# Scaled queries and a negated maximum for four blocks, and a new order of all engines, in windowed attention with a feed-forward network

## The chip, the cores and the metric

The kernel runs on one core of a Trainium2 chip, in one launch. The metric is the device time of one execution in microseconds (us), lower being better. The engines of a core work side by side, each through its own list of instructions in order: PE (TensorE: matmuls), DVE (VectorE), ACT (ScalarE), POOL (GpSimd) and SP (SyncE, which here only issues transfers). They wait for each other by semaphores.

## The reference

Attention with a sliding window of 128 keys and four sink keys, over 4 batches, 8 heads, 768 positions and 64 elements a head; its output, 3072 tokens of 512 elements, goes through a network of two layers.

```python
scores = scale * np.matmul(q, k.transpose(0, 1, 3, 2))     # scale = 1/sqrt(64)
keep = is_sink | in_window          # pos < 4, or 0 <= query - key < 128
scores = np.where(keep, scores, -1000000000.0)
scores = scores - np.max(scores, axis=-1, keepdims=True)
a = np.exp(scores)
a = a / (np.sum(a, axis=-1, keepdims=True) + 1e-09)
x = np.matmul(a, v)                 # then (4*768) x 512, heads side by side
h = x @ w_in                        # 512 x 2048
g = h * (1.0 / (1.0 + np.exp(-1.702 * h)))
out = g @ w_out                     # 2048 x 512
```

## The kernel before

The queries are cut into 24 blocks of 128, six to a batch; block b is the (b mod 6)-th of its batch. Blocks 0, 6, 12 and 18 are the first of their batches: they see one block of keys, their own, which contains the sinks. Every other block sees its own keys, those of the block before, and the four sinks. The blocks are worked on in the order 0, 6, 12, 18 and then the rest.

**Loads.** POOL issues the loads of q, k, v and of the two weight matrices (four slices each, `wi0` to `wi3` and `wo0` to `wo3`), which also cast float32 to float16. SP and ACT issue the loads of small constants: the identities `ident` and `identb`, the mask `bias0`, the mask `later`, and rows of v for the sinks (`vsa`). From `vsa`, `vsb` is made, one product for each batch (L344).

**A first block, step by step.** TensorE transposes q and k (`tq`, `tk`, L383), and DVE or ACT cast the results from PSUM into `qkT` (`cq`, `ck`). Four matmuls of `identb` with `bias0` write the mask into the PSUM buffer of the scores (`msk`, L464), and eight add the scores (`sc`, L478). DVE takes the maximum of each row (`mx`, L545), multiplies it by -scale (`nb`, L557), and ACT computes the exponential straight from PSUM with that bias, four instructions for each half of the heads (`bx`, L568). TensorE transposes the probabilities (`ta`, L650), they are copied (`ca`), multiplied with v, which has a column of ones (`av`, L710), normalised by DVE (`nm`, a reciprocal and a product, L722 and L723), transposed (`tx`, L740) and copied into `xT` (`cx`). The sinks' keys of a batch are copied out of `qkT` by DVE (`ks`, L446).

**The other blocks.** The mask is a predicated copy by DVE (`pk`, L535); the maximum is subtracted by DVE (`sb`, L582), and ACT takes one exponential for all heads out of SBUF (`ex`, L606). The sinks' scores come from matmuls of their own (`snk`, L507). From the fifth block on, q and k, the probabilities (`at<-a`, L681) and the attention output (`xT<-xn`, L753, called `txd`) are mostly transposed by DMA, issued by SP, and POOL separates the probabilities of the two key blocks (L637).

**The network.** Blocks form the groups [0], [6], [12, 18], and then pairs. For each group the first layer is computed in tiles (`h`, L786) and passed through the activation: for the first three groups by a tanh on ACT and a product on DVE (L800, L807), for the rest by one table function on ACT (`g`, L816). Where ACT goes from exponentials to this function or back, it loads a table (ACT_TABLE_LOAD). The second layer (`o`, L836) is copied from PSUM (`osb<-o`, by ACT or DVE) and stored by SP (L856). The last block is put out in two parts, of 320 and 192 columns.

**Buffers and order.** In PSUM three buffers (`mm`) serve all transposes, `hT` and `o`, two the scores and one `av`. Every step is an entry of a plan, and a list of numbers, ORDER, holds the sequence in which the steps are given to the engines; a letter behind a number chooses the engine where a step may run on several (d, a, p, s for DVE, ACT, POOL, SP). Each engine, and each engine's DMA queue, follows this sequence; nothing is decided while the program runs.

```python
    def emit(self, order):
        letter = {"d": DVE, "a": ACT, "p": POOL, "s": SP}
        ...
            op.emit(choice) if len(op.eng) > 1 else op.emit()
```

Of the kernel before, what the change touches and what calls it, by code (L numbers as in the profile page):

```python
# [40 lines left out]
LH = 1.0  # L41
HW = set()
LD4 = 0.65
LD, LW, QKX, ATX, XTX, STX, SPX2 = 0.97, 2.55, 1.55, 1.56, 0.77, 0.85, 1.9
AHEAD = 4
TQ = set(BLOCKS[:8])
# [5 lines left out]
RING = dict(RING,qkn=7)  # L52


ORDER = """
1a 9 6 8d 100 15 4a 5a 11 14 7 96 0a 23 94 21 3s 98 17 2s 29 18 104 107 105a 101p 102 103d 16 108 171 20 109 150 19
172a 10 95d 125 110 24 112 225 111 99d 26 151a 113 126d 27 114 115 97d 88 127 106 128a 130 92 226d 116a 117 12 90 129
148 118a 119 13 131 149a 22 120 194 132 121 86 196 195a 135 173 197a 87 133 122 134 89 123 199 124a 200 138 30 136 613
139d 137 25 152 142 174a 140 143 153 614 141d 615 154 91 144 155 619 156 145 157 158 146 616 93 620 147d 159 160 621
637 32 617 634 638 618 176 639 635 631 36 175 636 177 632 610 178 633 161 611 181 35 628 162a 179 612 180 163 182 165  # L60
622 164d 166 629 184 183 33 167 623 185d 168 39 198 630 169 31 204 640 170a 205 188 227 189 641 228a 201 28 230 186
206 642 231 209 202 624 187a 203 215 190 38 643 208 191 207 229 216d 210 644a 192 217 235 211 43 193a 625 232 212a 236
41 280 282 626a 256 281d 258 213 283a 627 233 652 259a 214 237 257a 649 653 218 238 234 261 661 241 40 650 262 654 239
285 37 260 651 662 242 286 304 44 655 266 243a 263 34 219 656 646 663 42 657 658 647 244 220 664 648 659 245 267 670
45 665 660 240 221 671 264 268 246 672 247a 269 265 248 667 222 270 249 666 250 284 668 271 251 48 676 669 46 290 252
323 673 47 253 287 677 291 254 306 272 678 288 255a 674a 223 292 679 273 224a 293 289 682 680d 294 51 307 305 683 50
688 295 308 311 49 686 309 675 52 684 687 312 689 692 310 685 313 276 693 690 314 277 296 315 704 297 344 324 345 705
327 691 316 53 330 325 694 326 361 331 274 695 696 275 328 698 697 681 332 278 317 699 279a 333 329 298 334 318 343
299 700 346 54 347 300 706 55 349 335 701 57 301 350 302 645 319 303a 707 348 702a 352 351 716 708a 320 353 362 336
321 717 354 720 322 337 365 724 709 59 721 363 399 714 364 368 60 712 715 703 369 725 722 366 713 340 355 723 710 341  # L70
367 718 711 356 371 370 338 719 732 64 339 372 726 342 56 733 62 382 381 373 61 383 727 387 384 359 734 360 385 728
388 401 735 390 386 729 374 419 389 750 402 391 375 730d 400 736d 751 748 392 67 406 403 742 66 404 752 65 743 407 749
740 63 753 378 738 379 408 376 739 744 377 393 409 357 405 745 746 358 741 394 420 380 747 439 58 410 754 440 423 421
760 422 426 397 755 427 411 398 761 424 457 756 425 762 428 757 429 430 412 766 758d 438 759 413 767 763 431 444 69
441 770 737 442 71 768 771 445 72 764a 772 769 446 68 416 443 773 780 432 447 417 788 781 433 448 414 774 415 73 458
459 789 775 460 449 464 395 778 396 461 776 418 779 465 782 777 462 436 495 450 783 463 466 790 75 765 437 731 784 467
74 468 434 451 785 435 476 791 482 786d 800 792a 479 454 793 801 798 469 455 794 514 452 795 802 453 808 803 456 477
804 809 478 470 799 483 796 480 471 806 797 485 805 484 816 76 481 810 77 486 474 80 496 475 817 70 502 807 499 487
497 82 811 498 78 500 818 503 81 516 822 504 819 823 505 517 501 812 820a 506 515 821 824 488 518 813 489 825 507 828
814d 83 472 826 552 473 79 519 832 827 521 829 535 836 833 536 522 492 837 834 508 523 830 524 493 509 520 844 831 84  # L80
835 490 534 525 491 845 540 494 541 838 537 846 526 542 839 538 512 787 847 513 543 840 539 544 553 852 848a 545 527
573 864 853 574 590 528 510 841 511 865 559 860 842d 529 546 861 556 862 530 850 547 554 854 851 555 85 560 531 855
856 532 557 858 533 857 561 866 859 558 550 815 562 591 563 551 872 597 867 863 592 564 873 593 598 868 843 594 548
849 880 595 869 596 881 600 565 888 599 549 874 889 870d 566 601 886 875 884 876a 602 567 885 572 568 878 877 575 569
879 892 570 578 882 571 893 603 576 887 890 579 604 894 891 577 883 900 580 581 895 582 901 607 912 608 583 896 913
605 871 897 606 902 898a 910 584 916 911 585 914 917 918 915 908 919 906 909 586 907 903 587 922 588 920 589 923 609
921 904a 928 924 929 925 930 926d 946 931 947 934 942 935 932a 948 943 933 940 905 927 936 941 899 938 937 949 944 939
956 945 950 957 951 958 952 962 953 963 954a 959 964 955 960d 965 961 966d 967
# [67 lines left out]
def kernel(  # L156
# [72 lines left out]
    z_s = plan.add("zs", DVE, 0.25, lambda: nc.vector.memset(vsa, 1.0), key=-897)  # L229
    z_a = [  # L230
# [133 lines left out]
    for pos, b in enumerate(BLOCKS):  # L364
# [5 lines left out]
        qkb = qkT[:, SLOT[b]]  # L370


        buf, n, unit = tunit[b]
        if b in OCT:
            parts = []
            before = used_slot.pop(SLOT[b], [])
            for w in (1, 0):
                tp = ps("mm", (P, 8, 4, 16), FP32, f"t{'qk'[w]}{b}")

                def t_qk(w=w, buf=buf, n=n, tp=tp):  # L380
                    for t in range(8):
                        for l in range(2):
                            nc.tensor.matmul(  # L383
                                tp()[64 * l : 64 * l + 64, t], buf()[:, n, w, t],
                                ident.rearrange("p (j l u) -> p l j u", l=2, u=16)[:, l], start=True, stop=True,
                            )
# [5 lines left out]
                parts.append(  # L392
                    plan.add(
                        f"c{'qk'[w]}{b}", {DVE: 0.6, ACT: 0.5}, 0,
                        lambda e, w=w, tp=tp, qkb=qkb: copy(
                            e, qkb[:, 4 * w : 4 * w + 4].rearrange("p c (u t) -> p c u t", t=8),
                            tp().rearrange("p t c u -> p c u t"),
                        ),
                        deps=[a] + before, give=[tp], key=K0 - 40,
                    )  # L400
                )
            o_qkt[b] = parts
        elif b in TQ:
# [3 lines left out]
            for w in (1, 0):  # L407

                def t_qk(w=w, buf=buf, n=n, tp=tp):
                    src = buf()[:, n, w].rearrange("p h d -> p (h d)")  # L410
                    for c in range(4):
                        nc.tensor.transpose(tp()[:, 4 * w + c], src[:, bass.ts(c, P)], ident)

                a = plan.add(
                    f"t{'qk'[w]}{b}", PE, 0.25 if early else 0.226, t_qk, deps=[ld["qk"[w], b], o_ident],
                    take=[tp], give=[buf], key=K0 - 40,
                )
                parts.append(
                    plan.add(
                        f"c{'qk'[w]}{b}", {DVE: 0.36, ACT: 0.49}, 0,  # L420
                        lambda e, w=w, tp=tp, qkb=qkb: copy(e, qkb[:, 4 * w : 4 * w + 4], tp()[:, 4 * w : 4 * w + 4]),
                        deps=[a] + before, give=[tp], key=K0 - 40,
                    )
                )
# [16 lines left out]
        if r == 0:  # L441

            def sink_keys(bb=bb, qkb=qkb):
                for hl in range(2):
                    rows = slice(64 * hl, 64 * hl + 64)
                    nc.vector.tensor_copy(  # L446
# [3 lines left out]
            o_ks[bb] = plan.add(f"ks{b}", DVE, 0.45, sink_keys, deps=o_qkt[b] + [z_k], key=K0 - 10)  # L450
# [79 lines left out]
        for hf in range(2):  # L530
# [12 lines left out]
            def rowmax(hf=hf, t=sc[hf], own=own, small=small, ms=ms):  # L543
                part = small[:, 4 * hf : 4 * hf + 4].rearrange("p (j l) -> p l j", l=2)
                nc.vector.tensor_reduce(out=part, in_=t()[:, :, :, own], axis=AX.X, op=ALU.max)  # L545
# [154 lines left out]
        for hf in range(2):  # L700
# [34 lines left out]
        if b in TX:  # L735
# [163 lines left out]
```

## Time and profile before

| | |
|---|---|
| time, median of 3 runs | 233.0 us (232.78 to 233.21) |
| profiled execution | 232.43 us |
| its span, first to last instruction | 230.7 us |
| TensorE busy | 217.0 us, 94% |
| VectorE busy | 154.5 us, 67% |
| ScalarE busy | 139.8 us, 61% |
| GpSimd busy | 111.2 us, 48% |
| first matmul starts | 5.68 us |

The profiled execution is one run of the program. An engine counts as busy while it executes, not while it waits, issues a transfer or branches. In rows of groups, the name behind an arrow (`<-`) at the end is what ended the engine's idle time; in the timeline the numbers are the start and the duration in us.

### The profile page before, as it was taken

The page shows a single profiled execution, that of the slowest core. Times are in us where ns is not written, and L with a number is a line of the kernel's source. Part 1 is how long each engine was busy: PE and PEld are TensorE (multiplying, and loading weights), DVE is VectorE, ACT ScalarE, POOL GpSimd, SP SyncE. Part 2 cuts the span into 40 slices and gives each one's busy share as a digit, 9 for nine tenths or more (in the row PEclk, how much of TensorE's full clock was granted, in tenths as well). Part 3 has the DMA queues.
Part 4 walks back from the last instruction along what each step waited for, and adds up shares of the span by engine and source line. Part 5 has one row for each costly group of instructions (what it writes and reads, how often), then busy time and mean ns, then how long its engine had stood idle before and what let it go on. Part 6 is the DMA issues. An engine that isn't in the chain of part 4 may idle for free. (4 is left out here: it accounts for less than half of the span.)

```text
span 230.7 us, 5431 instructions
## 1 busy us (share of the span) xinstructions
PE 217.0 (94%) x2202; PEld 151.6 (66%) x2202; DVE 154.5 (67%) x388; ACT 139.8 (61%) x220; POOL 111.2 (48%) x129
## 2 busy tenths in 40 slices
PE   0878899999999999999999999999999999999994
PEld 0666865876586686486577496486686686775863
DVE  2487899999979976987797848668577847121001
ACT  2278774874597687168378386786358486631531
POOL 8983435995393869077392619265350312300000
PEclk9999999999999999999999999999999999999999
DMA  5999999999999899999999989999647542402312
GB/s 76 167 189 200 206 198 180 168 134 91 153 182 168 159 242 131 148 162 135 165 196 136 196 172 131 131 185 110 140 92 114 142 99 45 99 0 45 114 71 91
DMA packets 120904, 32.07 MB, mean 139 GB/s; under 512 B 112016, under 2 KB 117936, under 8 KB 120880
## 3 DMA queue, kind: packets, MB, share of 16 engines
q0 software_dynamic: 69888, 13.64, 72.2%
q1 hardware_dynamic: 50512, 17.96, 38.7%
q8 instruction: 17, 0.28, 0.5%
q10 hardware_dynamic: 480, 0.13, 0.3%
q14 instruction: 7, 0.06, 0.1%
HBM read 27.46 MB, written 6.29 MB: 146 GB/s over the span
## 5 line engine op out<-in xcount | busy, mean ns | idle before, releaser
L786 PE MATMUL hT<-xT,w_in 128*128 128x256 f16 (+1 forms) x832 | 93.2, 264 | 1.5 <-ACT gT L816 0.5
L836 PE MATMUL o<-w_out,gT 128*128 128x512 f16 (+2 forms) x400 | 92.1, 371 | 0.0
L786 PEld LDWEIGHTS <-w_in 128*128 128x128 f16 x832 | 73.9, 98 | 14.1 <-issue 3.7
L816 ACT ACTIVATE gT<-hT 128x512 f16<-128x512 f32 x80 | 45.8, 597 | 33.1 <-PE hT L786 32.9
L836 PEld LDWEIGHTS <-gT 128*128 128x128 f16 x400 | 36.1, 98 | 33.3 <-issue 1.9
L637 POOL TENSOR_SCALAR_AFFINE_SELECT atp<-at 128x1024 f16<-128x1024 f16 (+1 forms) x22 | 22.3, 1015 | 72.9 <-DMA at<-a 69.9
L545 DVE TENSOR_REDUCE mx<-sc 128x4 f32<-128x512 f32 x48 | 32.7, 683 | 0.8 <-PE sc L478 0.5
L606 ACT ACTIVATE a<-e 128x1056 f16<-128x1056 f32 (+2 forms) x24 | 22.5, 938 | 15.4 <-issue 12.5
L535 DVE COPY_PREDICATED sc<-later,sc 128x512 f32<-128x512 uint16 x40 | 26.8, 689 | 3.6 <-PE sc L483 3.3
L582 DVE TENSOR_TENSOR e<-sc,mx 128x512 f32<-128x512 f32 x40 | 26.7, 684 | 0.7
L722 DVE RECIPROCAL rcp<-av 128x4 f32<-128x4 f32 x48 | 8.6, 179 | 24.0 <-PE av L712 22.1
L637 POOL TENSOR_SCALAR_AFFINE_SELECT at<-at 128x1024 f16<-128x1024 f16 (+1 forms) x22 | 22.2, 1009 | 1.4
L271 POOL DMA_DIRECT2D v<-in_v_dram x24 | 21.7, 906 | 2.0 <-DMA w_in<-in_moe_w_in_dram 1.2
L723 DVE TENSOR_TENSOR xn<-av,rcp 128x256 f16<-128x256 f32 x48 | 20.4, 424 | 1.7
L241 DVE COPY osb<-o 128x512 f32<-128x512 f32 (+2 forms) x10 | 6.3, 634 | 21.2 <-PE o L836 21.1
L606 ACT ACT_TABLE_LOAD x12 | 15.4, 1283 | 6.1 <-DVE e L596 4.0
L318 POOL DMA_DIRECT2D qkn<-in_q_dram x18 | 16.1, 897 | 4.5 <-DMA w_out<-in_moe_w_out_dram 1.6
L816 ACT ACT_TABLE_LOAD x13 | 16.7, 1283 | 2.4 <-PE hT L786 1.8
L318 POOL DMA_DIRECT2D qkn<-in_k_dram x18 | 16.0, 890 | 3.6 <-DMA w_out<-in_moe_w_out_dram 3.4
L710 PE MATMUL av<-v,at 128*128 128x65 f16 x192 | 17.5, 195 | 0.1
L710 PEld LDWEIGHTS <-at 128*128 128x128 f16 x192 | 14.4, 98 | 2.7 <-DVE at L241 0.3
L712 PE MATMUL av<-v,atp 128*128 128x65 f16 x160 | 15.1, 194 | 0.0
(58 smaller groups left out, 198.1 us busy)
## 6 DMA issues: line engine op xcount, KB each, us to landing
out_dram<-osb SPq DMA_DIRECT2D x23, 256.0 KB, 3.2
qkn<-in_q_dram POOLq DMA_DIRECT2D x24, 128.0 KB, 5.7
qkn<-in_k_dram POOLq DMA_DIRECT2D x24, 128.0 KB, 5.4
v<-in_v_dram POOLq DMA_DIRECT2D x24, 128.0 KB, 5.5
w_in<-in_moe_w_in_dram POOLq DMA_DIRECT2D x4, 512.0 KB, 10.4
w_out<-in_moe_w_out_dram POOLq DMA_DIRECT2D x4, 512.0 KB, 15.4
at<-a SPq DMA_TRANSPOSE x18, 3.7
qkT<-qkn SPq DMA_TRANSPOSE x10, 4.3
```

The costliest lines, as they stand in the source:

```text
L271: f"v{b}", POOL, 0.88, lambda b=b, view=view: nc.gpsimd.dma_start(v65[:, b, :, 0:D], view),
L318: lambda buf=buf, n=n, w=w, view=view: nc.gpsimd.dma_start(buf()[:, n, "qk".index(w)], view),
L535: nc.vector.copy_predicated(out=t()[:, :, :, own].rearrange("p l j s -> p (l j) s"), mask=later.unsqueeze(1).to_broadcast((P, 4, P)), data ...
L545: nc.vector.tensor_reduce(out=part, in_=t()[:, :, :, own], axis=AX.X, op=ALU.max)
L582: nc.vector.tensor_tensor(out=e32()[:, 512 * hf : 512 * hf + 512].rearrange("p (l j s) -> p l j s", l=2, j=2), in0=t()[:, :, :, own], in1= ...
L606: nc.scalar.activation(out=a16()[:, lo:hi], in_=e32()[:, lo:hi], func=AF.Exp, scale=scale)
L637: nc.gpsimd.affine_select(out=dst, in_=at()[:, lo : lo + num], pattern=[[0, num], [1 if own else -1, P]], compare_op=ALU.is_ge if own else ...
L710: nc.tensor.matmul(av()[:, i], at()[:, c], v65[:, b, h], start=(r == 0), stop=(r == 0))
L723: nc.vector.tensor_tensor(out=xn()[:, xi, 4 * hf : 4 * hf + 4].rearrange("p (j l) d -> p l j d", l=2), in0=av()[:, :, 0:D].rearrange("p (l ...
L786: nc.tensor.matmul(ht()[:, n].rearrange("p (n t) -> p n t", n=NT), w_in16[:, c, bass.ts(f, P)], t0()[:, i0 : i0 + NT, c], start=(c == 0), ...
L816: lambda fs=fs, gt=gt, ht=ht: nc.scalar.activation(out=gt()[:, fs[0] : fs[-1] + 1], in_=ht(), func=AF.Gelu_apprx_sigmoid),
L836: nc.tensor.matmul(po()[:, 0:width], gt()[:, F, bass.ts(t, P)], w_out16[:, F, c0 : c0 + width], start=(F == 0), stop=(F == NF - 1),)
```

## The change

For the four first blocks the cast of q now multiplies by scale, and the row maximum is written negated into the buffer from which the exponential takes its bias. The eight `nb` steps fall away, and the exponential has a scale of 1. `ks` may run on POOL. A constant tile of ones is set (`zo`), which no step of this kernel reads: the branch for it, a value product with the operands exchanged (AVT), is empty, as is OCTDT's other choice.

All of ORDER is new, and with it the choice of engines. TensorE has the same 328 steps in another sequence. SP issues `identb` and `bias0` before anything else (before, ACT issued them as third and fourth); `later` goes to ACT. `vsb` of batches 0 and 2 and one `ks` go from DVE to POOL; casts and evictions change places between DVE and ACT, so that DVE has 275 steps after 276, ACT 163 after 172, with 30 table loads in the program after 26, and POOL 128 after 125. On TensorE the start reads as follows, before and after (the last figure of `ta`, `av` and `h` is the half or the tile):

```
before: tq0 msk0 tk0 sc0 tk18 tq12 tk6 tk2 ta0_0 tq6 msk6 ta0_1 tk12 av0_0 sc6 tk1 av0_1 tq1 tq18 tx0 snk1 ta6_0 h0_1 ...
after:  msk0 tq0 tk0 sc0 tk18 tk1 tq6 tk6 tq18 msk6 ta0_0 sc6 ta0_1 tq12 tk12 av0_0 av0_1 ta6_1 msk12 ta6_0 tx0 sc12 tk2 h0_1 ...
```

The loads of POOL up to the last slice of `w_out`:

```
before: q0 k0 k18 q12 k6 k2 q6 v0 k12 v6 q18 k1 q1 wi1 wi3 wi2 v12 wi0 wo0 wo1 q2 v18 wo2 wo3
after:  q0 k0 k18 k1 q6 k6 k12 q18 q12 k2 v0 wi1 wi0 v6 q1 v12 wi2 q2 wi3 wo0 wo1 v18 wo2 wo3
```

The last four steps of TensorE were the last part of 320 columns and then that of 192; now the part of 320 columns ends the list, and ACT copies it. The diff, without the numbers of ORDER and the unused branch:

```diff
+OCTDT = "FP32"
+AVT = set()
+NEGATE = True
...
+    ones = const.tile([P, D], FP16, name="ones")
+    z_o = plan.add("zo", DVE, 0.12, lambda: nc.vector.memset(ones, 1.0), key=-890)
...
+        prescaled = NEGATE and b in NB
+        qf = [scale if prescaled else 1.0, 1.0]
...
-                        lambda e, w=w, tp=tp, qkb=qkb: copy(
+                        lambda e, w=w, tp=tp, qkb=qkb, qf=qf: copy(
                             e, qkb[:, 4 * w : 4 * w + 4].rearrange("p c (u t) -> p c u t", t=8),
-                            tp().rearrange("p t c u -> p c u t"),
+                            tp().rearrange("p t c u -> p c u t"), qf[w],
                         ),
...
-            def sink_keys(bb=bb, qkb=qkb):
+            def sink_keys(e, bb=bb, qkb=qkb):
...
-                    nc.vector.tensor_copy(
+                    (nc.vector if e == DVE else nc.gpsimd).tensor_copy(
...
+            def rowmax(hf=hf, t=sc[hf], own=own, small=small, ms=ms, neg=prescaled):
                 part = small[:, 4 * hf : 4 * hf + 4].rearrange("p (j l) -> p l j", l=2)
+                if neg:
+                    nc.vector.tensor_reduce(out=part, in_=t()[:, :, :, own], axis=AX.X, op=ALU.max, negate=True)
+                    return
...
-                    nbias = const.tile([P, 8], FP32, name=f"nb{b}")
+                    nbias = small if prescaled else const.tile([P, 8], FP32, name=f"nb{b}")
...
-                o = plan.add(f"nb{b}_{hf}", DVE, 0.09, neg, deps=[o], key=K0 - 29)
-
-                def bexp(hf=hf, t=sc[hf], own=own, a16=a16, nbias=nbias):
+                if not prescaled:
+                    o = plan.add(f"nb{b}_{hf}", DVE, 0.09, neg, deps=[o], key=K0 - 29)
+
+                def bexp(hf=hf, t=sc[hf], own=own, a16=a16, nbias=nbias, scale=1.0 if prescaled else scale):
```

More of the change, by code (lines that the diff above doesn't have):

```diff
@@ L45 @@
 AHEAD = 4
+AVT = set()
+NEGATE = False
 TQ = set(BLOCKS[:8])
@@ L60 @@
[L60 to L64, printed above, removed]
@@ L420 @@
                         f"c{'qk'[w]}{b}", {DVE: 0.36, ACT: 0.49}, 0,
-                        lambda e, w=w, tp=tp, qkb=qkb: copy(e, qkb[:, 4 * w : 4 * w + 4], tp()[:, 4 * w : 4 * w + 4]),
+                        lambda e, w=w, tp=tp, qkb=qkb, qf=qf: copy(
+                            e, qkb[:, 4 * w : 4 * w + 4], tp()[:, 4 * w : 4 * w + 4], qf[w]
+                        ),
                         deps=[a] + before, give=[tp], key=K0 - 40,
@@ L734 @@
         xt, ti = xts[b]
-        if b in TX:
+        if b in AVT:
+            pass
+        elif b in TX:
             tpx = ps("mm", (P, 4, P), FP16, f"tx{b}")
```

98 lines of the change are left out of this document (65 added, 33 removed).

## The prediction

> **What bounds the kernel now.** The page comes first: what each engine does in the span.
>
> ```profile
> span 230.7 us, 5431 instructions
> PE 217.0 (94%) x2202; PEld 151.6 (66%) x2202; DVE 154.5 (67%) x388; ACT 139.8 (61%) x220; POOL 111.2 (48%) x129
> ```
>
> TensorE works 217.0 of 230.7 us, so 13.7 us are all that a reordering can win; its matmuls are the same 2202 after the change. The profiled execution took 232.43 us, 1.7 beyond its span; the median of the runs is 233.0 (232.78 to 233.21), 0.6 above it. I make the sum against the execution and carry the difference over to the median. The table by stages (columns: stretch and length, then PE, PEld, DVE, ACT and POOL busy, clock, DMA share, GB/s) says where the 13.7 us lie.
>
> ```profile
> 5.77:11.50 5.73, 4.62 (x108) 3.72 (x109) 2.79 (x7) 1.64 (x4) 5.73 (x8) 1.00 1.43 167
> 11.50:17.30 5.80, 4.60 (x76) 3.54 (x76) 4.74 (x14) 4.44 (x13) 5.18 (x8) 1.00 1.36 189
> 17.30:23.00 5.70, 4.95 (x99) 3.83 (x98) 4.32 (x16) 4.69 (x13) 2.01 (x3) 1.00 1.37 200
> 23.00:28.80 5.80, 5.14 (x87) 4.66 (x86) 4.65 (x13) 4.29 (x13) 2.50 (x3) 1.00 1.29 205
> 28.80:34.60 5.80, 5.63 (x80) 4.04 (x74) 5.41 (x15) 4.20 (x12) 1.75 (x2) 1.00 1.42 198
> 60.00:220.00 160.00, 159.05 (x1455) 109.75 (x1454) 105.81 (x262) 102.39 (x136) 71.30 (x73) 1.00 1.04 136
> 220.00:230.70 10.70, 7.65 (x55) 4.87 (x52) 0.85 (x2) 1.75 (x4) 0.00 (x0) 1.00 0.16 58
> ```
>
> TensorE loses 1.11, 1.20, 0.75, 0.66 and 0.17 us in the five stretches up to 34.6 (3.9 in all), 0.95 in the long one, and 3.05 behind its last matmul. The rest lies ahead of its first matmul, where it waits for the first load. Everything that the change can win stands in three numbers, then: start 3.9, middle 0.95, tail 3.05. The start moves 167 to 205 GB/s all along: the loads keep it company and may be its true limit.
>
> **The start, step by step.** Rows of the timeline, those between left out (start, us, engine, line, operation; in brackets the idle time before and what ended it), and of four groups (busy us, mean ns | idle time before, and what ended it):
>
> ```profile
> 2.14 0.75 ACTq L217 DMA_DIRECT2D bias<-cbias  x1
> 5.68 0.64 PE L383 MATMUL tq<-ident,qkn 128*64 128x64 f16 x16 [5.68 <-DMA qkn<-in_q_dram]
> 6.60 1.01 PE L464 MATMUL sc<-bias,identb 128*128 128x256 bf16 x4 [0.28 <-DMA bias<-cbias]
> 7.54 0.64 PE L383 MATMUL tk<-ident,qkn 128*64 128x64 f16 x16
> 8.97 0.61 PE L478 MATMUL sc<-qkT 64*128 64x128 f16 x8 [0.79 <-DVE qkT L241]
> 9.40 0.69 DVE L545 TENSOR_REDUCE mx<-sc 128x4 f32<-128x512 f32 x1 [0.49 <-PE sc L478]
> 11.03 1.14 ACT L568 ACTIVATE a<-sc,nb 128x128 f16<-128x128 f32 x4 [0.26 <-DVE nb L557]
> 20.04 1.05 PE L786 MATMUL hT<-xT,w_in 128*128 128x128 f16 x16 [0.24 <-ACT xT L245]
> 41.51 1.03 PE L836 MATMUL o<-w_out,gT 128*128 128x512 f16 x4
> L557 DVE TENSOR_SCALAR nb<-mx 128x4 f32<-128x4 f32 x8 | 1.7, 208 | 0.0
> L568 ACT ACTIVATE a<-sc,nb 128x128 f16<-128x128 f32 x32 | 9.3, 390 | 2.0 <-DVE rcp L722 1.7 <-DVE nb L557 0.3
> L241 DVE CAST qkT<-tk 128x512 f16<-128x512 f32 x3 | 2.1, 685 | 5.0 <-PE tk L383 4.9
> L239 DVE TENSOR_SCALAR osb<-o 128x512 f32<-128x512 f32 x1 | 0.7, 679 | 0.0
> ```
>
> The arithmetic change itself is small. It removes eight `nb` of 208 ns, 1.7 us of VectorE, and puts nothing in their place, if a maximum that is written negated and a cast that also multiplies cost what they did without (the trace of before shows neither; a copy of the same size that scales is there in one output eviction, 679 ns against the plain cast's 685, so I take 0, with +0.1 us an instruction, eight maxima and four casts, 1.2 us of VectorE, as the far end). On the path the eight are worth far less than 1.7: ScalarE waited for `nb` 0.3 us in all. At the first block 0.94 us lie between the end of the maximum (9.40 + 0.69) and the exponential (11.03), and that gap closes by at most that much.
>
> The order does more. `identb` and `bias0` are now issued by SyncE first of all, not as third and fourth of ScalarE's queue (2.14), and the four mask matmuls stand ahead of `tq0` on TensorE. Where the two constants land before the 5.6 us of q, the mask is paid inside the first wait, and `tk0` starts at 6.22 and not 7.54. Where they land late, the mask delays `tq0` instead; the gain is then near 0.4. I take the early case: `sc0` at 7.73, 1.24 earlier. From there each step waits for something that did not move: the transposes of k of block 18 for a free product buffer, at 10.4, whose cast waits for a load; `tq18` for q's load, 11.9; the mask of block 12 for the exponentials of block 6, 17.3; `tx0` for the cast of q of block 12, 18.4. The first matmuls of the network start at 19.4 against 20.04, with one block's mask and scores more behind them. (These starts come from walking the new order by hand with the rows' durations and the loads in their order.) The loads come in the same number ahead of the last slice of `w_out`, and this one bounds the first output blocks:
>
> ```profile
> 24.04 0.74 POOL L331 DMA_DIRECT2D w_out<-in_moe_w_out_dram  x1 [1.79 <-DMA w_in<-in_moe_w_in_dram]
> ...
> DMA to landing us min/median/max: 14.9/15.4/15.9
> L344 POOL TENSOR_TENSOR vsb<-vsa,ownm 32x520 f16<-32x520 f32 x1 | 1.2, 1227 | 0.0
> ```
>
> It lands at 24.04 + 15.4 = 39.4, and the fourth output tile of block 0 cannot start before; by my chain it starts at 39.85. Before it starts at 41.51, but with one more output tile (0.86 us of spacing) and one set of transposes (0.22) behind it, so that at equal work the new order stands at 40.93: **0.6 us gained** of the 3.9. Behind it the transposes of blocks 4 and 3 wait for casts of q and k, 0.2 given back: **start -0.4**. The two `vsb` products that go to GpSimd take 1.2 us each there and delay the loads issued behind them; as the last slice stands 15.4 us in the queue, the queue does not run dry, and I cost that at 0 (2.5 us of late loads, if it did).
>
> **The middle.** The program loads ScalarE's tables 30 times where it was 26, as some pairs of exponentials are now apart.
>
> ```profile
> L816 ACT ACTIVATE gT<-hT 128x512 f16<-128x512 f32 x80 | 45.8, 597 | 33.1 <-PE hT L786 32.9
> L816 ACT ACT_TABLE_LOAD x13 | 16.7, 1283 | 2.4 <-PE hT L786 1.8 <-PE snk L507 0.3
> 142.04 1.28 ACT L606 ACT_TABLE_LOAD   x1 [1.47 <-issue]
> 146.38 1.03 PE L786 MATMUL hT<-xT,w_in 128*128 128x256 f16 x8 [0.55 <-ACT gT L816]
> ```
>
> Four more loads are 5.1 us of ScalarE by the row, and up to 4 x (1.28 + 1.47) = 11 with the idle time ahead of the load shown. ScalarE waits 32.9 us for `hT`, so that much is covered in sum; if the cover fails at one place, TensorE loses what it lost at 146.38, 0.55 us. One stop in 13 switches of this kind before makes 0.2 for four more. (The Trainium skill, "ScalarE: Activation LUTs", section "What ACT_TABLE_LOAD costs", gives 1283 ns and a drain of about 1380 ns for each switch, and so speaks against this change with 10.6 us of ScalarE. The trace agrees with the first part exactly; for the second it has the 1.47 us of idle time, which stand ahead of the load and not behind it.)
>
> The DMA transposes on SyncE's queue (of the attention output, `txd`) have less TensorE work to hide behind. The one ahead of group 5 shows the danger:
>
> ```profile
> 90.24 1.32 SPq L753 DMA_TRANSPOSE xT<-xn  x1
> 97.52 0.70 PE L786 MATMUL hT<-xT,w_in 128*128 128x256 f16 x5 [0.34 <-DMA xT<-xn]
> xT<-xn SPq DMA_TRANSPOSE x8, 3.1
> ```
>
> It took 7.3 us where the median is 3.1, and cost 0.34. Between the last value product of that group and its first network matmul lie 8.4 us of TensorE work before and 6.0 after (counted in the two orders with the trace's spacings); for the groups after it 8.4 against 7.2 and 8.5 against 5.1. At the median's 3.1, with 0.6 of normalising and up to 0.8 of queue ahead, that is 4.5, and all hold, with 0.6 to 2.7 us left. Around this transpose four loads were issued before, one now. So I drop most of the 0.95 us of stops, leave 0.45 for the new ones and the table loads: **middle -0.5**.
>
> **The tail.** The last output tile is now the one of 320 columns, evicted by ScalarE, not that of 192 by VectorE:
>
> ```profile
> 227.08 0.96 DVE L241 COPY osb<-o 128x320 f32<-128x320 f32 x2 [14.31 <-PE o L836]
> 227.69 0.36 DVE osb L241
> out_dram<-osb SPq DMA_DIRECT2D x23, 256.0 KB, 3.2
> out_dram<-osb SPq DMA_DIRECT2D x1, 96.0 KB, 1.7
> ```
>
> The eviction grows by about 0.1 us, and the store from 96 to 160 KB: between the rows (64 of 160 KB more, of 1.5 us) 0.6, though those of 256 KB met other traffic; I take 0.2 for it, 0.1 to 0.7 in all. **Tail +0.3.**
>
> Sum: -0.4 - 0.5 + 0.3 = -0.6; 231.8 on the execution's footing, **232.4 against the median's 233.0**.
>
> **The rivals.**
>
> *A transpose lands late (slower).* Had the first `txd` taken as long as before, with 6.0 in place of 8.4 us beside it, TensorE would stop 0.34 + 2.4 = 2.7 us instead of 0.34. It decides where a landing passes some 4.5 us from issue. For it: the 7.3 us in the row, three places where up to 40% of the cover is gone. Against: the loads that were issued around it have moved away. Time: 232.4 + 2.7 = 235.1; half of it, 233.8.
>
> *TensorE warms up later (slower).* The same four mask matmuls take 1.03 us at 13.78 and 0.60 at 21.28:
>
> ```profile
> 13.78 1.03 PE L464 MATMUL sc<-bias,identb 128*128 128x256 bf16 x4
> ...
> 21.28 0.60 PE L464 MATMUL sc<-bias,identb 128*128 128x256 bf16 x4
> ```
>
> In the new order TensorE has a gap of about 1 us at 16 to 17 (value products of block 0 wait for a normalisation, the mask of block 12 for exponentials). If that moves the fast state behind the first network matmuls, the mask costs 0.43 more and 16 such matmuls 0.86 more: +1.3, of which the waits absorb little; 233.7. (The Trainium skill, "TensorE: Matmul & The Clock Gate", "What's actually happening", has the clock doubled after a busy window of about 3.4 us whose phase runs free. The change of the row agrees, though the granted clock in the table by stages reads 1.00 throughout; no run here shows the window.)
>
> *The loads bound the start.* Had `w_out` always been the limit, or `bias0` landed late, the 0.4 is gone and the casts' 0.2 stays: 233.0.
>
> *All stops go.* Start -1.0 as several waits close at once, middle -0.95, tail +0.1: 231.1.
>
> That the change brings nothing by its arithmetic alone is part of the forecast: 0.3 us is its whole price on the path.
>
> **How the numbers follow.** Forecast 0.40 (231.8 to 232.9), all stops go 0.12, loads 0.13, late transposes 0.24, late warm-up 0.11. About 0.2%, 0.47 us, is what a measurement of this kernel can tell from no change. Faster by that means under 232.53: three quarters of the forecast's case less a little, all of the second, a little of the third: 0.28 + 0.12 + 0.03 = 0.43. Within: 0.10 of the forecast's and 0.07 of the loads' case and 0.01 of the rest: 0.18. Slower: 0.39. The range reaches from 230.7 (start -1.3, middle -0.95, tail 0) to 235.1, the late transpose in full; 1 in 8 is left out.
>
> **What would show it.** Right: `sc0` near 7.7, the first network matmul near 19.4, the fourth `o` tile of block 0 at 39.4 to 40, no `nb` rows; in the long stretches TensorE idle under 0.5 us; the last store about 0.3 us longer behind its matmul. Wrong: the list of TensorE's waits names `xT<-xn` or `atp` with over 1 us (late transposes), the masks of blocks 12 and 18 both at 1.0 us (late warm-up), or casts of q that take 0.1 us more than the 0.6 to 0.7 of before (a scaling that is not free).

## The result and the profile after

The changed kernel takes 235.6 us (median of 6 runs, 234.48 to 236.27) against 233.1 for the kernel before (232.65 to 233.54): a ratio of 1.0105, 95% interval 1.0077 to 1.0132. It is slower by 1%, where 232.4 was forecast and 235.1 was the end of the range. Run again beside later kernels, it took 236.4 (ratio 1.0144, 1.0104 to 1.0185). Every ratio is to the kernel before, run in the same batch, and is formed from the runs within 1.5% of the fastest of their kernel; where a kernel has others (one run in ten with the stores moved, two in ten with the reductions in the new order), the median given is of all runs and up to 0.3 us higher than theirs.

The page of the changed kernel, first lines:

```profile
span 233.6 us, 5436 instructions
## 1 busy us (share of the span) xinstructions
PE 219.2 (94%) x2202; PEld 153.3 (66%) x2202; DVE 157.2 (67%) x387; ACT 139.9 (60%) x214; POOL 113.6 (49%) x133
```

The span grew by 2.9 us. VectorE has eight instructions of `nb` fewer and yet 2.7 us more busy time. What TensorE waited for, without the first loads and the waits of 0.2 us or less (us in total, times, longest):

```profile
PE hT L835 <- DVE osb L247: 1.3, 1, 1.3
PE tq L391 <- DVE qkT L245: 0.9, 1, 0.9
PE sc L488 <- DVE qkT L247: 0.8, 1, 0.8
PE av L757 <- DVE xn L770: 0.7, 1, 0.7
PE tx L789 <- ACT at L251: 0.5, 1, 0.5
PE hT L835 <- ACT osb L251: 0.5, 1, 0.5
PE av L752 <- DVE ss L530: 0.3, 1, 0.3
```

`xT<-xn` is not among them: no transpose by DMA came late. In their place stand evictions (`osb`) and the sink copy `ss`, which the forecast had not on its list; the other four fall in the start, before 26 us. The two late stops in the table by stages:

```profile
160.00:180.00 20.00, 19.39 (x180) 12.44 (x179) 17.02 (x43) 16.46 (x20) 7.39 (x7) 1.00 0.61 87
180.00:200.00 20.00, 20.00 (x182) 13.69 (x180) 7.34 (x21) 8.70 (x12) 4.37 (x4) 1.00 0.35 61
200.00:220.00 20.00, 18.72 (x144) 13.38 (x141) 2.43 (x5) 6.16 (x12) 0.00 (x0) 1.00 0.33 73
```

To compare orders I use one number, TensorE's delay: the start of a step less the undisturbed spacings of all steps ahead of it (for each kind of step, the median spacing in the trace of before). It grows where TensorE waits or runs at its slow clock, and not with work. Each row is one execution, and these differ: the profiled ones took, from the top, 232.4, 235.4, 236.8, 233.7, 233.9, 232.8 and 231.7 us, and that of the changed kernel with reductions is 2 us faster than its median. From the profiles:

| delay of TensorE, us, at | 45 us | 100 us | 160 us | 227 us |
|---|---|---|---|---|
| before | 13.7 | 15.4 | 17.2 | 17.5 |
| changed | 14.6 | 16.4 | 17.4 | 20.2 |
| changed, run again | 14.2 | 17.4 | 18.4 | 21.7 |
| stores moved up | 13.5 | 16.6 | 17.6 | 18.6 |
| stores and two subtractions moved up | 14.2 | 16.1 | 17.7 | 18.8 |
| changed, with reductions | 14.0 | 15.2 | 16.2 | 17.7 |
| before, with reductions | 14.0 | 15.2 | 16.5 | 16.8 |

So in this execution the 2.9 us are 0.9 up to 45 us, 1.8 from there to 227, and 0.2 behind the last matmul (the span ends 3.23 us behind it, 3.05 before). The 1.8 are a gain and a loss: from 100 to 160 us the delay grows by 1.0 where it grew by 1.8 before, as old stops are gone, and from 160 to 227 by 2.8 where it grew by 0.3.

### The profile page after: what moved, and what is told of

Read it like the earlier page. It is cut to its first block, busy times and chain, and to the rows that moved or that the text cites. A ratio compares the mean times of both kernels' runs of the same rounds, so it can differ in the third digit from the quotient of the medians.

```text
span 233.6 us, 5436 instructions
## 1 busy us (share of the span) xinstructions
PE 219.2 (94%) x2202; PEld 153.3 (66%) x2202; DVE 157.2 (67%) x387; ACT 139.9 (60%) x214; POOL 113.6 (49%) x133
## 4 chain that ended last, share of the span: by engine, by line
PE 69%; DVE 17%; ACT 6%; DMA 4%; issue 2%; POOL 0%; DVEq 0%; ACTq 0%; POOLq 0%
PE hT L835 29%; PE o L885 26%; DVE sc L545 3%; PE sc L493 3%; DVE mx L558 3%; DVE e L596 2%; DMA qkn<-in_k_dram 2%; PE av L757 2%; DMA out_dram<-osb 2%; DVE xn L770 2%; ACT a L620 2%; ACT L865 2%; DVE gT L856 2%; PE av L752 1%; PE av L759 1%
## 5 line engine op out<-in xcount | busy, mean ns | idle before, releaser
L835 PE MATMUL hT<-xT,w_in 128*128 128x256 f16 (+1 forms) x832 | 94.7, 265 | 2.2 <-DVE osb L247 1.3
L885 PE MATMUL o<-w_out,gT 128*128 128x512 f16 (+2 forms) x400 | 93.2, 371 | 0.0
L865 ACT ACTIVATE gT<-hT 128x512 f16<-128x512 f32 x80 | 45.1, 597 | 40.2 <-PE hT L835 39.7
L247 DVE COPY osb<-o 128x512 f32<-128x512 f32 x13 | 9.0, 689 | 30.1 <-PE o L885 26.1
L558 DVE TENSOR_REDUCE mx<-sc 128x4 f32<-128x512 f32 x40 | 27.3, 682 | 0.2
L770 DVE TENSOR_TENSOR xn<-av,rcp 128x256 f16<-128x256 f32 x48 | 20.4, 424 | 1.7
L757 PE MATMUL av<-v,at 128*128 128x65 f16 x192 | 17.6, 196 | 0.7 <-DVE xn L770 0.7
## 6 DMA issues: line engine op xcount, KB each, us to landing
w_out<-in_moe_w_out_dram POOLq DMA_DIRECT2D x4, 512.0 KB, 13.7
```

Source lines behind the costliest of these rows:

```text
L757: nc.tensor.matmul(av()[:, i], at()[:, c], v65[:, b, h], start=(r == 0), stop=(r == 0))
L770: nc.vector.tensor_tensor(out=xn()[:, xi, 4 * hf : 4 * hf + 4].rearrange("p (j l) d -> p l j d", l=2), in0=av()[:, :, 0:D].rearrange("p (l ...
L835: nc.tensor.matmul(ht()[:, n].rearrange("p (n t) -> p n t", n=NT), w_in16[:, c, bass.ts(f, P)], t0()[:, i0 : i0 + NT, c], start=(c == 0), ...
L865: lambda fs=fs, gt=gt, ht=ht: nc.scalar.activation(out=gt()[:, fs[0] : fs[-1] + 1], in_=ht(), func=AF.Gelu_apprx_sigmoid),
L885: nc.tensor.matmul(po()[:, 0:width], gt()[:, F, bass.ts(t, P)], w_out16[:, F, c0 : c0 + width], start=(F == 0), stop=(F == NF - 1),)
```

## The experiments

**The arithmetic and the order, one at a time.** First the change's arithmetic in the order of before (the eight `nb` taken out of the list, the memset of ones put in early):

```diff
-... mx0_0 nb0_0 ... bx0_0
+... mx0_0 ... bx0_0        # before's ORDER, NEGATE = True
```

> The arithmetic alone: the order of before with queries scaled in their cast and the maximum written negated, the eight negations left out. Theory (the new order is what costs): the time of before, within 0.3 us, 232.8 to 233.3, since the exponentials waited only 0.3 us for the negations in all. Rival (the arithmetic costs: the scaled cast or the negated maximum is dearer, or moves the start): 1 us or more above before, and casts of q or maxima that take longer than 0.6 and 0.69 us.

Measured: 232.99 us, ratio 0.9994 (0.9975 to 1.0013). The theory holds. The groups show why: the negated maximum costs 681 ns, where a plain one took 0.69 us in the forecast's row, and the scaled cast on ScalarE 621 where the plain one costs 585.

```profile
L249 ACT ACTIVATE qkT<-tq 128x512 f16<-128x512 f32 x4 | 2.5, 621 | 2.5 <-PE tq L391 2.5
L251 ACT CAST qkT<-tq 128x512 f16<-128x512 f32 x2 | 1.2, 585 | 0.9 <-PE tq L391 0.8
L556 DVE TENSOR_REDUCE mx<-sc 128x4 f32<-128x512 f32 x8 | 5.4, 681 | 0.5 <-PE sc L488 0.5
```

Then the new order with the old arithmetic:

```diff
-NEGATE = True
+NEGATE = False             # after's ORDER, nb<b>_<half> behind each mx<b>_<half>
```

> The new order alone: the changed kernel with the eight negations put back behind their maxima and unscaled queries. Theory (the order costs): as slow as the changed kernel, 235.4 to 236.2, ratio to before 1.010 to 1.013, the same three stops of TensorE late in the span. Rival (the arithmetic costs): back near 233.1.

Measured: 238.8 us, ratio 1.0232 (1.0182 to 1.0281): slower than the two measurements of the change by 2 to 3 us, which neither side expected. The eight negations that are worth nothing in the old order are dear in the new one: ScalarE's exponentials now wait for them, and the negations themselves take longer (347 ns against 208). The two rows of the timeline show one of them, which ends with an instruction of GpSimd.

```profile
L570 DVE TENSOR_SCALAR nb<-mx 128x4 f32<-128x4 f32 x8 | 2.8, 347 | 0.3
L582 ACT ACTIVATE a<-sc,nb 128x128 f16<-128x128 f32 x32 | 9.0, 377 | 3.2 <-DVE nb L570 3.0
15.91 1.17 POOL L350 TENSOR_TENSOR vsb<-vsa,ownm 32x520 f16<-32x520 f32 x1
16.55 0.56 DVE L570 TENSOR_SCALAR nb<-mx 128x4 f32<-128x4 f32 x1
```

3.0 us in place of 0.3. So the two halves of the change can't be added up: arithmetic 0 alone, order +5.7 alone, both +2.5 to +3.3. How these waits become the 2 to 3 us at the end was not followed.

**The loads.** `vsb` moved behind the loads on GpSimd:

```diff
-vsb0p (behind q18)  vsb2p (behind v6)  vsb3p (behind v12)
+wo3 vsb0p vsb2p vsb3p
```

> The changed kernel with the three products vsb of batches 0, 2 and 3 moved on GpSimd behind the issue of the last slice of w_out; nothing else. Theory (these products, 3.5 us of GpSimd between the issues of loads, let the load queue run thin from 10 to 17 us, 129 to 145 GB/s where before had 173 to 206): the rate between 12 and 17 us comes back to 170 or more, the last slice of w_out lands near 39.4 instead of 40.9, and the first output tiles come up to 1 us earlier; 234.6 to 235.2. Rival (the rate is that of the two weight slices themselves, or the late clock sets the start): landing at 40.9 still, time unchanged at 235.6.

Measured: 236.2 us, ratio 1.0145 (1.0085 to 1.0204). Half of the theory holds: between 12 and 17 us the loads move 186 GB/s (last column) where the changed kernel had 135.

```profile
12.00:17.00 5.00, 4.16 (x71) 3.19 (x71) 3.33 (x8) 2.07 (x7) 3.73 (x6) 1.00 1.32 186
```

But the last slice of `w_out` lands at 40.25 (40.9 in the changed kernel, 40.1 in the kernel with the stores moved below, 38.6 in the changed kernel's second profile, which is no faster for it), and the time doesn't fall. Nothing here shows the loads setting the time, and costing the move of `vsb` at nothing stands.

**The stop at 205.8.** Rows of the changed kernel's timeline:

```profile
199.84 0.69 DVE L247 COPY osb<-o 128x512 f32<-128x512 f32 x1 [1.08 <-PE o L885]
200.56 0.33 SPq L905 DMA_DIRECT2D out_dram<-osb  x1
201.11 1.41 SPq L802 DMA_TRANSPOSE xT<-xn  x1
202.58 1.74 SPq L905 DMA_DIRECT2D out_dram<-osb  x2
205.10 0.69 DVE L247 COPY osb<-o 128x512 f32<-128x512 f32 x1 [4.01 <-DMA out_dram<-osb]
205.84 0.38 PE L835 MATMUL hT<-xT,w_in 128*128 128x256 f16 x2 [1.28 <-DVE osb L247]
```

VectorE stands 4.0 us before it can evict block 17, because all four output buffers are taken: those of blocks 13, 15, 16 and 19, evicted from 166 to 200 us, of which SyncE's new list stores 19 first (200.56) and 15 and 13 only behind a transpose (202.58). TensorE then wants the PSUM buffer that this eviction frees. The repair:

```diff
-tat23 st14_ ... tat22 ... txd21 ... st19_ txd23 st15_ ev17_ st13_
+tat23 st13_ st14_ ... tat22 st15_ ... txd21 ... st19_ txd23 ev17_
```

> The changed kernel with two stores moved up on SyncE's queue: that of block 13 ahead of block 14's, that of block 15 ahead of the transposes for group 11, so that their two output buffers come free before the eviction of block 17. Theory (the 1.3 us stop at 205.8 is the eviction waiting 4.0 us for one of four output buffers): that stop goes, the time falls by 1.2 to 1.5 us, to 234.1 to 234.4. Rival (the stop is the eviction's own lateness, or the stores moved up delay the transposes that follow by as much): 235.3 or more, a wait for xT or at in its place.

Measured: 235.1 us, ratio 1.0058 (1.0026 to 1.009). The stop is gone (TensorE's delay grows by nothing at 205 us, 18.5 to 18.6 from 190 to 227), the eviction of block 17 starts at 202.61, so the cause of this stop is shown. What it is worth in time is less certain: 0.5 to 1.4 us by the medians against the two measurements of the change. The time expected, 234.1 to 234.4, was not reached, and the interval of the ratio still touches that of the change (1.0077 to 1.0132).

**The stop at 166.9.** It was first put down to ScalarE's order:

```diff
-ex20 ... ev13_a
+ev13_a ex20
```

> The changed kernel with one exponential on ScalarE, that of block 20, moved behind the eviction of block 13; nothing else. Theory (the first late stop of TensorE, 0.47 us at 166.9, comes from an eviction that stands behind an exponential and that exponential's own table load): the stop goes, and TensorE stands 0.5 to 0.9 us earlier from there on; 234.7 to 235.1. Rival (the exponential was the more urgent of the two): a new wait for at or for the value products of block 20 of the same size; 235.6 or more.

Measured: 237.9 us, ratio 1.0178 (1.0128 to 1.0227). The rival holds, and by more than it said. The eviction now stands at the head of ScalarE's list, which waits for it, and the exponential behind it is late by 3.4 us:

```profile
166.76 0.58 ACT L251 COPY osb<-o 128x512 f32<-128x512 f32 x1 [4.61 <-issue]
167.37 1.28 ACT L620 ACT_TABLE_LOAD   x1
168.66 1.08 ACT L620 ACTIVATE a<-e 128x1056 f16<-128x1056 f32 x1
...
171.71 1.03 PE L835 MATMUL hT<-xT,w_in 128*128 128x256 f16 x8 [1.43 <-ACT gT L865]
```

**TensorE's clock.** Matmuls without a use, while the first loads are awaited:

```diff
+wm: 18 x matmul(av buffer, ones, ones, 256 columns), first in TensorE's list
```

> The changed kernel with 18 matmuls of 256 columns on a tile of ones ahead of the first mask, into a buffer that the first value product overwrites; they run while the first loads are awaited. The fast state of TensorE then comes before 10 us in every run, not at 15 in some and at 22 in others. Theory (VectorE, 94 to 98% busy from 28 to 63 us, sets when the fourth group's first layer can go on, whatever TensorE gained before): the first network matmul near 20 and the last output tile of block 0 at 40 or before, 1.2 us earlier than in the changed kernel's profile, but a longer stop near 65, and the same time, 235.2 to 235.7. Rival (the late warm-up, forecast at 1.3 us, is lost for good): 234.0 to 234.6.

Measured: 235.2 us, ratio 1.0082 (1.0048 to 1.0117). The first premise fell: the full clock came early and was lost again. The mask of block 0 runs at 0.60 us, that of block 6 at 1.03, that of block 18 at 0.60 again:

```profile
4.81 0.60 PE L481 MATMUL sc<-bias,identb 128*128 128x256 bf16 x4
6.38 0.44 PE L398 MATMUL tq<-ident,qkn 128*64 128x64 f16 x16 [0.96 <-DMA qkn<-in_q_dram]
8.20 0.61 PE L495 MATMUL sc<-qkT 64*128 64x128 f16 x8 [1.03 <-DVE qkT L254]
12.96 1.03 PE L481 MATMUL sc<-bias,identb 128*128 128x256 bf16 x4
23.47 0.60 PE L481 MATMUL sc<-bias,identb 128*128 128x256 bf16 x4
8.00:12.00 4.00, 2.88 (x72) 2.46 (x72) 3.25 (x9) 2.42 (x9) 4.00 (x6) 0.51 1.34 167
```

The last row is of the table by stages; its third number from the right is the granted clock, 0.51. The time lies in the theory's range, but by luck: the start was not quicker (the first network matmul came at 21.15), so the theory was not tried. The same matmuls in the kernel before:

> The kernel before with 18 matmuls of 256 columns on a tile of ones at TensorE's start, as in the run with the same matmuls in the changed kernel, where the fast state came at 4.6 us and was lost at 8. Theory (a start that is quicker is taken back by VectorE up to 65 us): 232.8 to 233.3, the time of before. Rival (the slow clock of the start costs the kernel its 1.2 us at the end too): 231.8 to 232.4 if the fast state holds.

Measured: 233.9 us, ratio 1.0021 (0.9994 to 1.0047): no gain, but no test of the clock either. In its profile the full clock is lost as well, and TensorE waits 1.1 us at 33.86 for a slice of `w_out`. What a slow start costs at the end isn't settled by these two. In the profiles of two kernels with the same start, the last matmuls at the slow clock start at 21.4 us in the changed kernel and near 16 in the one with the stores moved, whose delay at 45 us is 1.1 lower; at 100 us it is 0.2 higher. That looks as if a quicker start were spent by then, but 0.7 of this 1.3 has another cause: one subtraction, shown below, that took 1.86 us there and 1.15 in the changed kernel.

**VectorE's load.** Six copies go from VectorE to ScalarE:

```diff
-ca1_0d ca1_1d cq4d ck4d ck3d ev18_d
+ca1_0a ca1_1a cq4a ck4a ck3a ev18_a
```

> The changed kernel with six copies between 41 and 63 us given from VectorE to ScalarE (two of transposed probabilities of block 1, three casts of q and k of blocks 4 and 3, one eviction, 2.7 us of VectorE). Theory (VectorE is the pace there): the stop near 65 us shrinks and TensorE passes the value products of block 8 up to 1 us earlier than at 95.5; 234.6 to 235.3. Rival (the pace is TensorE's own, or the loads'): no change at 65 and at 95.5; 235.4 to 235.9.

Measured: 237.3 us, ratio 1.0167 (1.0115 to 1.022). Not so: TensorE now waited for ScalarE's casts (0.40 us at 45.7, 0.21 at 48.8), and the stops at 66 and 96 stayed (0.30 and 0.48). With this, the two repairs above and an earlier sink copy in one kernel:

> All repairs together in the changed kernel: the two stores moved up, the exponential of block 20 behind the eviction of block 13, six copies to ScalarE, and the sink copy of block 11 ahead of two maxima on VectorE, so that the one buffer of the value products comes free earlier. Theory (four separate places make up the loss): 1.4 + 0.7 + 0.5 to 1.0 us less than the changed kernel, 232.4 to 233.2, as fast as before or a little faster. Rival (each stop that goes opens another): 234 or more.

238.1 us, ratio 1.02 (1.0159 to 1.024). The rival holds; the run contains two moves that are harmful alone, so it says little more than they do.

**Small operations that last as long as a select.** In the changed kernel's timeline two subtractions of 128x32, 0.18 us elsewhere, stand out:

```profile
91.42 1.11 POOL L651 TENSOR_SCALAR_AFFINE_SELECT at<-at 128x1024 f16<-128x1024 f16 x1
91.43 1.15 DVE L610 TENSOR_TENSOR e<-ss,mx 128x32 f32<-128x32 f32 x1
...
95.29 0.18 DVE L530 COPY ss<-snk 128x32 f32<-128x32 f32 x1
95.52 0.27 PE L752 MATMUL av<-vsb,at 128*128 128x260 f16 x1 [0.28 <-DVE ss L530]
...
162.80 1.09 POOL L651 TENSOR_SCALAR_AFFINE_SELECT atp<-at 128x1024 f16<-128x1024 f16 x1 [5.71 <-DMA at<-a]
162.96 0.97 DVE L610 TENSOR_TENSOR e<-ss,mx 128x32 f32<-128x32 f32 x1
164.00 1.28 ACT L620 ACT_TABLE_LOAD   x1 [2.86 <-issue]
166.28 0.57 ACT L251 COPY osb<-o 128x512 f32<-128x512 f32 x1
166.90 1.03 PE L835 MATMUL hT<-xT,w_in 128*128 128x256 f16 x8 [0.47 <-ACT osb L251]
```

Both end within 0.05 us of a select on GpSimd. Behind the first, VectorE works without a pause until the sink copy that frees the buffer of the value products; behind the second comes the exponential of block 20, and behind that the eviction. In the thirteen profiles of kernels with this form, 144 of the small operations with two operands in SBUF (`e<-ss,mx` and `mx<-mx,ms`) started while a select ran: 136 ended within 0.06 us of its end, and the other eight had started in its last 0.08 us and took their usual 0.16 to 0.18. The operations beside a select that read one operand from SBUF, or one from PSUM, did not stretch so. Selects are not the only neighbours that hold VectorE up. In the changed kernel's second profile the subtraction of block 9 starts while GpSimd issues a load (91.54 to 92.43) and ends with the select behind it:

```profile
91.74 1.86 DVE L610 TENSOR_TENSOR e<-ss,mx 128x32 f32<-128x32 f32 x1
92.43 1.12 POOL L651 TENSOR_SCALAR_AFFINE_SELECT at<-at 128x1024 f16<-128x1024 f16 x1
96.54 0.27 PE L752 MATMUL av<-vsb,at 128*128 128x260 f16 x1 [0.99 <-DVE ss L530]
```

Most of the small operations that start while GpSimd issues a load keep their time, some do not. And beside instructions other than selects one operand is no protection for every form: the negation above took 0.56 us beside the `vsb` product, and a copy of sinks' keys in the same profile 1.20. The two subtractions moved up in VectorE's list, with the stores:

```diff
-nm7_1 ssb9 ...   sb20_0 ... nm19_1 ... ms21 ssb20
+ssb9 nm7_1 ...   sb20_0 ssb20 ... nm19_1 ... ms21
```

> The changed kernel with the two stores moved up (as in the run of the stores) and two small subtractions on VectorE (of the sinks' scores, 128x32, blocks 9 and 20) moved up by one or three steps in VectorE's list, so that they no longer start beside the selects of GpSimd that start at 91.42 and 162.80 in the changed kernel. There they took 1.15 and 0.97 us instead of 0.18 and ended within 0.05 us of the select's end, and the wait of the value products of block 8 and the late eviction of block 13 follow them. Theory (a small VectorE operation with both operands in SBUF stands until GpSimd's select is done, and this is what makes the stops at 95.5 and 166.9): the subtractions take 0.2 us, both stops shrink by 0.5 us or more in sum, 233.4 to 234.4, at least 0.6 below the run of the stores alone. Rival (the stops come from the order itself): the stops stay, 234.8 or more.

> The changed kernel once more, unchanged, beside the others. 235.3 to 236.0; the stops at 65, 95, 166 and 206 us again, of other sizes where they hang on which small operation meets a select; the last one (an output buffer that is not free) within 0.3 us of its 1.3.

Measured: 234.0 us, ratio 1.004 (1.001 to 1.0071), and the unchanged changed kernel beside it 236.4 (1.0144), above its range, with all its stops again and the last of them at 1.3 as expected. Both stops are gone in the repaired one: the value products of block 8 start at 95.24 without a wait, and the eviction of block 13 stands ready before its matmuls end. Four profiles side by side (us) show that the stops follow the subtractions:

| | subtraction of block 9 | wait of value products | subtraction of block 20 | wait behind eviction |
|---|---|---|---|---|
| changed | 1.15 | 0.28 | 0.97 | 0.47 |
| changed, run again | 1.86 | 0.99 | 1.09 | 0.59 |
| stores moved up | 1.86 | 0.99 | 0.18 | none |
| stores and two subtractions moved up | 1.20 | none | 0.18 | none |

Where the first takes 0.71 longer, the wait is 0.71 longer. With the stores alone moved, the subtraction of block 20 happened to start 0.01 us ahead of the select and took 0.18, and the second stop is missing. One detail of the repair missed: the subtraction of block 9 met a GpSimd issue and another select in its new place, but there VectorE had time. The price in time of the two subtractions alone is not clear of noise: the interval overlaps that of the stores alone (1.0026 to 1.009).

**The form of the operation.** The 40 maxima as reductions:

```diff
-nc.vector.tensor_tensor(out=part, in0=part, in1=ms[:, 4 * hf : 4 * hf + 4], op=ALU.max)
+nc.vector.tensor_reduce(out=part, in_=pair[:, 4 * hf : 4 * hf + 4, 0:2], axis=AX.X, op=ALU.max)
```

`pair` holds a block's own maximum and that of the sinks side by side; the work and its place in the order are the same.

> The changed kernel with another form of one small operation on VectorE and nothing else: the 40 maxima of a block's own maximum with that of the sinks (mx<-mx,ms, 128x4) become reductions over pairs that lie side by side, so that each has one operand in SBUF where it had two. Theory (a VectorE operation with two SBUF operands stands until GpSimd's select is done; one with a single operand does not): none of the 40 takes over 0.25 us, where in the changed kernel some took up to 1.4 us beside a select; about 2 us of VectorE come free, the time falls by 0.3 to 1.2 us, to 234.4 to 235.5; the subtractions e<-ss,mx keep their long cases. Rival (the operations are slow because GpSimd fills SBUF's bandwidth, whatever their form): the reductions are stretched as often.

Measured: 234.7 us, ratio 1.0059 (1.0027 to 1.009), 0.9 to 1.7 below the two measurements of the change. The groups of before, of the changed kernel (lines 561 and 610) and of this one (lines 564 and 613):

```profile
L548 DVE TENSOR_TENSOR mx<-mx,ms 128x4 f32<-128x4 f32 x40 | 10.6, 265 | 1.4
L596 DVE TENSOR_TENSOR e<-ss,mx 128x32 f32<-128x32 f32 x20 | 5.5, 276 | 0.2
```

```profile
L561 DVE TENSOR_TENSOR mx<-mx,ms 128x4 f32<-128x4 f32 x40 | 8.9, 222 | 1.4
L610 DVE TENSOR_TENSOR e<-ss,mx 128x32 f32<-128x32 f32 x20 | 7.6, 379 | 0.1
```

```profile
L564 DVE TENSOR_REDUCE pair<-pair 128x4 f32<-128x8 f32 x40 | 6.4, 161 | 1.4
L613 DVE TENSOR_TENSOR e<-ss,pair 128x32 f32<-128x32 f32 x20 | 5.1, 257 | 0.1
```

In the changed kernel the subtractions alone take 2.1 us more than before. The reductions take 0.16 us each: of 160 in four profiles 26 started beside a select, and none was stretched, though each handles twice the elements, while subtractions in the same kernels still were (up to 1.10). So it is the form of the operation, and not the neighbour's traffic as such. (The Trainium skill, "SBUF — State Buffer", section "SBUF: two separate sides", states this: VectorE and GpSimd share a pair of ports, an exclusive lock held for a whole instruction, which a VectorE operation with two SBUF inputs needs beside a GpSimd operation that reads SBUF. The traces agree for the selects, and give it a price in this kernel.)

> The run with two stores and two subtractions moved up, with these reductions too. Theory: 0.2 to 0.8 us below that run's 234.0, 233.2 to 233.8, about the time of before. Rival (what is left is the order's own): 234.0 or more.

Measured: 232.9 us, ratio 0.9999 (0.9975 to 1.0022): the new order, repaired in these places, is as fast as before, a little better than the theory's range.

> The old order with the change's arithmetic (the run of the arithmetic alone) and these reductions. Theory (the old order is held up by the same collisions, of which its profile shows five among these maxima, 3.7 us in all, most of them off the path): 232.2 to 232.9, a little under before's 233.1. Rival (they cost the old order nothing): 232.9 to 233.2.

> The kernel before with these reductions alone. Theory: 232.4 to 233.0. Rival: 233.0 to 233.3. Beside the run with the arithmetic it tells whether the eight negations are worth anything to the old order once VectorE is less disturbed: 0.3 us or less.

Measured: 232.45 us, ratio 0.9955 (0.9931 to 0.9979), with the change's arithmetic, and 232.2, ratio 0.9957 (0.9936 to 0.9978), without it. The first theory holds, and the second too, with a time 0.2 under its range: the old order gains 0.45%, and the negations are worth nothing to it. The kernel before with the 40 reductions beats both kernels of this case.

## Why the prediction was wrong, point by point

**The account.** By the ratios, the new order with the reductions is 2.4 us slower than the old one with them (1.0059 against 0.9957), and without them 2.5 to 3.4 (1.0105 and 1.0144). The stretched maxima cost about 1.0 in the old order and 1.1 to 2.0 in the new one, then, and are not most of the difference. Two stores and two subtractions in other places take 1.4 of the 2.4 (0.9999 against 1.0059). Some 1.0 stays, 0.2 of it the tail; which steps hold the rest was not separated. Each ratio is good to 0.5 to 0.9 us, so these are sizes and not exact shares.

**The arithmetic, costed at 0: right**, in the old order. That the new order would depend on it by 2 to 3 us, the forecast did not see; it needed no sum for it, as both came together.

**The start, -0.4: wrong, +0.9 in the profile (+0.5 in the second one).** One premise held: `bias0` landed at 3.53, and the mask was paid inside the first wait. But the first load, issued at the same moment as before, landed at 6.27 and not 5.63 (5.89 in the second profile), so `sc0` came at 8.48 where 7.7 was forecast; the first network matmul came at 21.4 and the fourth output tile of block 0 at 41.38, against 19.4 and 39.4 to 40. The rival of the late warm-up is what this profile shows, by half of its sign: the mask of block 12 is slow, that of block 18 no longer.

```profile
18.46 1.06 PE L474 MATMUL sc<-bias,identb 128*128 128x256 bf16 x4
21.42 1.53 PE L835 MATMUL hT<-xT,w_in 128*128 128x128 f16 x16
24.00 0.60 PE L474 MATMUL sc<-bias,identb 128*128 128x256 bf16 x4
```

Its forecast +1.3 is about the 1.1 between this start and that of the kernel with the stores moved (20.4 and 40.2), and is what lies between -0.4 and the +0.9. How much of a start's gain or loss is left at the end, which the sum took for all of it, stays open: the delay that the change has more than before is 0.9 at 45 us and 0.2 at 160, but other stops come and go in between.

**The middle, -0.5: this is the step that failed.** It measured +1.8. That old stops would go was right (0.8 gained from 100 to 160 us); that only 0.45 of new ones would come was wrong (2.5 lost from 160 to 227). The list of what could stop TensorE held transposes by DMA and table loads, since those had stopped it before. Neither did in this profile. The transposes kept their time with the shorter cover (the slack of 0.6 to 2.7 us sufficed), and the four further table loads were covered as costed. What stopped TensorE was on no list: stores that were put behind others on SyncE's queue and kept their output buffers, a stop of 1.3 us, and operations of VectorE that a select held up, stops of 0.47 and 0.28. The first could have been read from the two lists of stores and evictions, since the eviction that needs a fifth buffer is in them; SyncE's queue was followed for transposes alone. The second stood in the profile of before, in two groups with means of 265 and 276 ns, of operations that take 0.16 and 0.18 us when nothing is beside them; which of them a new order puts beside a select, and on the path, could not be read there.

**The tail, +0.3: right**, 0.18 by the profile.

**The rivals.** The slow side was given 0.39, by a late transpose (no) and a late warm-up (seen at the start; its share of the end is open). The range ended at 235.1 and the time was 235.6.

## What to carry to other kernels

When an order is new, follow every ring of buffers through it, output buffers and their stores too: list who takes the next buffer and which transfer must have ended, as for the transposes. In a group of small operations compare the mean with the shortest; where it is far above, look what the neighbour does at the moments of the long ones, and change the operation's form before moving it. Whether a gain at the start lasts must be read further on; a sum that carries it to the end unchanged is a guess.

## What the runs showed of the hardware

A VectorE operation of 0.16 to 0.18 us whose two operands lie in SBUF took up to 1.15 us beside a GpSimd select of 1.1, ending with it, and 1.86 where it began during GpSimd's issue of a load, 0.7 ahead of the select. The same maximum as a reduction over one operand took 0.16 in all 160 cases, and 40 of these gave 1.0 us of 233. One operand alone was no protection for every form: a negation of 0.16 us took 0.56 beside a GpSimd product. TensorE's full clock, reached by 4.8 us through work without a use, was gone at 8.2 us, after idle stretches of 1.0 us each (before 6.4 and before 8.2), and did not come back until some 22 us, at a granted clock of 0.50 meanwhile.
